# Long convolution and linear attention in one kernel: the second inverse step without its DRAM turn, x turned on TensorE, and a new order of all instructions

## The chip, the cores and the metric

The kernel runs on one core of one Trainium2 chip. The metric is device time in microseconds: 200.88 us, the median of three runs (199.52 to 201.84). The engines are PE (TensorE: matmul, with its weight loads as PEld), DVE (VectorE), ACT (ScalarE), POOL (GpSimd) and SP (SyncE, which here only issues transfers). They run side by side, each in the order of its own queue, and wait for each other through semaphores. SBUF is the on-chip memory, PSUM the eight banks of 512 fp32 columns that matmuls write.

## What is computed

Two independent parts, whose outputs lie side by side in the last dimension (S = 2048 rows, D = 576 channels each, bf16).

```python
# A: y = q * (causal_long_conv(kv, ssm_k) + kv * ssm_D)
k_shift = sum(k_pad[:, t:t + S] * shift_k[:, ks - 1 - t] for t in range(4))
kv = k_shift * v
y = irfft(rfft(pad(kv, 2*S)) * rfft(pad(ssm_k, 2*S)))[:S].astype(bf16)
a = q * (y + kv * ssm_D)
# B: linear attention, 32 heads of 18 channels
q, k, v = split(x @ wqkv)
pq, pk = phi(q), phi(k)          # phi(t) = (t + 1 if t > 0 else exp(t)) + 1e-6
kv, z = pk^T v, sum(pk)          # per head
b = (pq kv) / (pq z + 1e-6) @ wo
out = concatenate([a, b], axis=-1)
```

## The kernel before

**Part A** takes the channels in three groups of 192 (`cc`). `conv_piece` makes kv on DVE from shifted copies of k: two products with four taps (L383), sums (L388, L391), and the product with v (L394), for the two halves of the rows (`bh` 0 and 1). `h_piece` turns ssm_k on TensorE (L416). The Fourier transform of the filter ("h") and of kv ("u") goes in two steps. `s1` multiplies by the table `Gsb` (L445): each step fills three PSUM banks, 1,536 columns, which ACT or DVE copies to SBUF (`copy`, L246 to L250, so that all these copies stand under L248 for ACT and L250 for DVE). `s2` transposes 32x32 blocks on DVE (L463) and multiplies with the 16-point matrix W, as 32x32 matmuls on four row groups and four column groups of the array (L476), two PSUM banks a step; 64 channels at a time, so nine pieces `g`.

`inv` multiplies the two spectra on DVE (`p1` L503, `p2` L500, the second with the filter's real and imaginary rows exchanged by a transfer, `X`), and applies the first inverse step as 32x32 matmuls with W stationary (L513). Its result V has the frequency in the free dimension. `inv2` therefore writes V to DRAM (`v_scr`) and reads it back with the frequency on the partitions (`Vt`: four reads for every four row offsets, 32 in all), multiplies with the table `Esb` (L550), multiplies the PSUM result with q on DVE (L555), and stores. It does so in two halves, of 320 and 256 channels.

**Part B** loads x transposed with transposing transfers (L299, L302), projects k (`kproj`, L577; exp on ACT L582, phi on DVE L585) and q (`qproj`, L599, L603, L606: two PSUM banks, 1,024 rows a step, transposed as pqT). `b_G` forms x^T pk (L636), and from it come kv per head, z, the matrix M = kv wo (`b_M`) and the denominators for all heads and rows, one matmul group (L712). Their reciprocal is one DVE instruction (L723). It is spread over the 18 channels of each head by 20 small matmuls into PSUM (`b_bc`, L747) and multiplied into pqT on DVE (L753, ten times). `b_out` multiplies pqT with M for 16 tiles of 128 rows (L766), two PSUM banks each, copies (`oev`) and stores (`oo`).

**The order** is written out. Every call of `P.op` records one step, and `PLAN` lists the steps of all engines in one sequence, each with a letter for its engine (P, A, D, G = POOL, S = SP) and its number; `_issue` reads it. `PLACES` gives each buffer's address or PSUM bank. No engine looks ahead: a step that waits holds up all that stands behind it in its own queue. Every transfer of the kernel is issued by SP, and it also takes one of eight completion counters in turn, so that it is not issued before the eighth transfer ahead of it has landed.

The loads that the prediction speaks of: `kh0` holds rows of k in blocks of 16 per partition, with the three rows ahead of each block in the columns 0 to 2. These three rows are loaded apart (`khh`, L332 and L334), as 15 and as 112 partitions, and both for 192 and for 384 channels.

Of the kernel before, what the change touches and what calls it, by code (L numbers as in the profile page):

```python
# [14 lines left out]
D = 576  # L15
EPS = 1e-6
FT = [0, 128, 256, 384, 449]
HCH = [(0, 126), (126, 126), (252, 126), (378, 126), (504, 72)]
HEADS = [7, 7, 7, 7, 4]
CC = 192  # L20
NCC = 3
PCH = 64
VN = (320, 256)
VP = (0, 5)
HALF = 288

class Buf:

    def __init__(self, name, shape, dt=BF, space="sb", side=0, banks=0, pre=False):
        self.name, self.shape, self.dt, self.space = name, list(shape), dt, space
        self.side, self.banks, self.pre = side, banks, pre
        n = 1
        for d in shape[1:]:
            n *= d
        self.nbytes = -(-n * (4 if dt == FP32 else 2) // 32) * 32
        self.users = 0
        self.pos = None
        self.keys = {}  # L40
        self.t = None
# [6 lines left out]
class Prog:  # L48
# [11 lines left out]
    def op(self, engs, fn, rd=(), wr=(), name="", bias=0.0, tx=0.0, after=(), use=(), cnt=1):  # L60
        o = Op()
        o.id = len(self.ops)
        o.engs = engs if isinstance(engs, dict) else dict([engs])
        o.fn, o.name, o.bias, o.tx, o.cnt = fn, name, bias, tx, cnt
# [28 lines left out]
        for b in use:  # L93
            note(b)
# [3 lines left out]
        for b in bufs:  # L98
            b.users += 1
# [19 lines left out]
def _tables():  # L119
# [11 lines left out]
    pp = np.arange(128)  # L131
    k2p = 32 * (pp % 4) + pp // 4
    phe = ((4 * k2p[:, None, None] - 1) * n.T[None, :, :]) % 8192
    E = np.empty((128, 16, 2, 128), np.float32)
    E[:, :, 0, :] = np.cos(w0 * phe) / 2048.0
    E[:, :, 1, :] = -np.sin(w0 * phe) / 2048.0
# [17 lines left out]
    W[np.abs(W) < 1e-7] = 0.0  # L154

    C = np.zeros((128, 96 + 128 + 630 + 32 + 160 + 126 + 8), np.float32)
    o = 0
    C[:, 0:96] = np.tile(W.reshape(32, 96), (4, 1))
    o = 96
    C[:, o:o + 128] = np.eye(128)  # L160
    o += 128
    es = np.zeros((32, 5, 126), np.float32)
    hm = np.zeros((128, 5, 32), np.float32)
    for c, (h0, hn) in enumerate(HCH):
        for m in range(hn):
            es[7 * c + m // 18, c, m] = 1.0
            hm[m, c, 7 * c + m // 18] = 1.0
    C[:, o:o + 630] = np.tile(es.reshape(32, 630), (4, 1))
    o += 630
# [8 lines left out]
    return G.astype(bf), E.astype(bf), C.astype(bf)  # L178
# [10 lines left out]

def _pe(*ns):
    return sum(max(n / 2400.0, 0.026) + 0.0025 for n in ns)

def _act(n):
    return 0.17 + n * 0.000868

def _dve(n, rate=1):
    return 0.145 + n * 0.001045 / rate  # L200

def _dma(nb, row=4096):
    return nb / (16.0 * row / (8.0 + row * 0.0412) * 1000.0)
# [3 lines left out]
def kernel(  # L208
# [17 lines left out]
    Gt, Et, Ct = _tables()  # L226
    G_d = nc.inline_tensor(Gt.reshape(128, -1), name="tab_g").ap()
    E_d = nc.inline_tensor(Et.reshape(128, -1), name="tab_e").ap()
    C_d = nc.inline_tensor(Ct, name="tab_c").ap()

    V_d = [nc.dram_tensor("v_scr%d" % i, (128, 32 * VN[i]), BF, kind="Internal").ap() for i in range(2)]
# [7 lines left out]
    def dma(dst, src):  # L239
        nc.sync.dma_start(out=dst, in_=src)  # L240

    def load(name, b, fn, nb, wr=None, rd=(), bias=0.0, after=(), issue=0.45, row=4096):
        return P.op(("SP", issue), fn, rd=rd, wr=[b] if wr is None else wr, name=name, bias=bias,
                    tx=_dma(nb, row), after=after)

    def copy(e, o, i):  # L246
        if e == "ACT":
            nc.scalar.activation(out=o, in_=i, func=ACTF.Copy)  # L248
        else:
            nc.vector.tensor_copy(out=o, in_=i)  # L250

    def either(n, da=0.0, dd=0.0, rate=1):
        return {"ACT": _act(n) + da, "DVE": _dve(n, rate) + dd}
# [5 lines left out]
    cst = SB("cst", [128, Ct.shape[1]], side=1, pre=True)  # L259
    neg1 = SB("neg1", [128, 1], FP32, side=1, pre=True)  # L260
    Gsb = SB("Gsb", [128, 16, 2, 128], side=1, pre=True)
    Esb = SB("Esb", [128, 16, 2, 128], side=1)
# [3 lines left out]
    wk = SB("wk", [128, 5, D], side=1, pre=True)  # L266
    wq = SB("wq", [128, 5, D], side=1, pre=True)
    Drow = SB("Drow", [1, D], side=1)
    x_sb = SB("x_sb", [128, 16, D + 1], side=1)
    pk = SB("pk", [128, 16, D + 1], side=1, pre=True)  # L270
    pqT = SB("pqT", [128, 5, S], side=1, pre=True)
# [4 lines left out]
    W2 = lambda: cs(0, 32)  # L276
    W31 = lambda: cs(32, 32)
    W32 = lambda: cs(64, 32)
    ident = lambda: cs(96, 128)
    esel = lambda: cs(224, 630).rearrange("p (c m) -> p c m", c=5)  # L280
    sel127 = lambda: cs(854, 32)
    hmask = lambda: cs(886, 160).rearrange("p (c m) -> p c m", c=5)
    maskbd = lambda: cs(1046, 126)
    epsc = lambda: cs(1172, 1)

    P.op(("POOL", 0.1), lambda e: nc.gpsimd.memset(neg1.t[:], -1.0), wr=[neg1], name="neg1", bias=1000)
    for wx in (wk, wq):
        P.op(("POOL", 0.4), lambda e, wx=wx: nc.gpsimd.memset(wx.t[0:64, 4, :], 0.0), wr=[(wx, "z")], name="wz", bias=990)
        P.op(("POOL", 0.4), lambda e, wx=wx: nc.gpsimd.memset(wx.t[0:1, 4, :], 1.0), rd=[(wx, "z")], wr=[(wx, "z")],
             name="w1", bias=980)  # L290
# [3 lines left out]
    def xt_load(g):  # L294
        b = SB("xT%d" % g, [128, 5, 512])
# [5 lines left out]
        def f2(e):  # L301
# [580 lines left out]
```

## Time and profile before

The runs took 200.88, 201.84 and 199.52 us. The profiled execution has a span of 197.3 us from its first to its last instruction; its own time is not listed, so what lies around the span is taken as the 3.6 us to the median.

| what | value |
|---|---|
| median of three runs | 200.88 us |
| span of the profiled execution | 197.3 us |
| PE busy | 162.8 us, 83%, 1,664 matmuls |
| DVE busy | 153.4 us, 78%, 150 instructions |
| ACT busy | 120.0 us, 61%, 127 instructions |
| POOL busy | 6.9 us, memsets only |
| mean granted TensorE clock | 0.895 of full speed |
| transfers | 39.49 MB; SP alone issues |

A group of the profile has a source line, an engine, an operation, the tiles' names with their shapes, a count, and then the busy time and the mean duration of one; behind the second bar stands how long the engine was idle just before such instructions, and what ended that. In a row of stretches stand the stretch, its length, and per engine the busy time and number of instructions. The chain is followed back from the last instruction to what released each step.

### The profile page before, as it was taken

Reading aid. Unit: us, or ns where it says so; the run is one execution under the profiler, and the core shown is the slowest. Engines: PE = TensorE matmul, PEld = TensorE weight load, DVE = VectorE, ACT = ScalarE, POOL = GpSimd, SP = SyncE. Lnnn points to the kernel's source line nnn. Section 1 sums busy time; section 2 is a strip of 40 time slices with the busy share of each in tenths; the row PEclk is TensorE's granted clock in tenths of the full one; section 3 lists DMA queues with packets and bytes.
Section 4 is the critical chain, followed back from the end, with each engine's and each line's share of the span. In section 5 each row is a group of like instructions: output and inputs, shape, how many; then the busy total and the mean of one; then the engine's idle time right before and its main releaser. Section 6 shows DMA issues by size and latency. Waiting matters only on the chain.

```text
span 197.3 us, 3955 instructions
## 1 busy us (share of the span) xinstructions
PE 162.8 (83%) x1664; PEld 108.2 (55%) x1664; DVE 153.4 (78%) x150; ACT 120.0 (61%) x127; POOL 6.9 (3%) x18
## 2 busy tenths in 40 slices
PE   0985999938999999889998897798779999996820
PEld 0763576627666675668775564362233566774610
DVE  0477599999799999999954999979899548482650
ACT  2293566595767576997524699979998583201100
POOL 8010100020010000000000000000000000000000
PEclk9996699985999999999999999769555699999996
DMA  6999899996013680209950021930699789967696
GB/s 182 348 171 262 307 379 382 300 230 138 0 22 118 201 279 17 92 3 278 372 233 0 3 106 69 308 108 0 257 342 257 187 240 360 354 189 211 198 323 185
DMA packets 40536, 39.49 MB, mean 200 GB/s; under 512 B 13575, under 2 KB 37765, under 8 KB 39622
## 3 DMA queue, kind: packets, MB, share of 16 engines
q1 hardware_dynamic: 40518, 39.24, 64.7%
q8 instruction: 13, 0.21, 0.5%
q14 instruction: 5, 0.04, 0.1%
HBM read 22.46 MB, written 9.44 MB: 162 GB/s over the span
## 4 chain that ended last, share of the span: by engine, by line
PE 37%; DVE 24%; ACT 12%; SPq 11%; issue 7%; DMA 6%; DVEq 1%; ACTq 0%
PE ps_all L636 8%; SPq L240 7%; PE ps_all L599 6%; PE ps_all L577 6%; PE ps_all L766 6%; DVE m L383 5%; PE ps_all L445 5%; DMA Vt<-v_scr 3%; ACT Cu L248 3%; DVE X L500 3%; SPq L299 2%; DVE pk L585 2%; DVE ct L463 2%; DMA wk<-in_B_wqkv_dram 2%; PE ps_all L550 2%
## 5 line engine op out<-in xcount | busy, mean ns | idle before, releaser
L445 PEld LDWEIGHTS <-Gsb 128*128 128x128 bf16 x240 | 20.0, 113 | 11.2 <-issue 9.7
L577 PE MATMUL ps_all<-wk,xT 128*128 128x288 bf16 x160 | 23.4, 306 | 2.5 <-DMA wk<-in_B_wqkv_dram 2.5
L766 PE MATMUL ps_all<-M,pqT 126*128 126x288 bf16 (+1 forms) x160 | 23.5, 305 | 0.2 <-ACT V L248 0.2
L599 PE MATMUL ps_all<-xT,wq 128*126 128x512 bf16 (+1 forms) x100 | 23.5, 386 | 0.1
L383 DVE TENSOR_TENSOR m<-kh,Wj 128x3072 bf16<-128x3072 bf16 x12 | 20.7, 1750 | 1.9 <-DMA kh<-in_A_k_dram 1.9
L577 PEld LDWEIGHTS <-xT 128*128 128x128 bf16 x160 | 16.4, 104 | 9.3 <-issue 3.6
L766 PEld LDWEIGHTS <-pqT 126*128 126x128 bf16 (+1 forms) x160 | 16.4, 103 | 7.5 <-issue 2.2
L636 PE MATMUL ps_all<-pk,x_sb 128*128 128x288 bf16 (+1 forms) x160 | 20.4, 286 | 0.1
L248 ACT ACTIVATE sph<-ps_all 128x1024 bf16<-128x1024 f32 x16 | 16.2, 1028 | 4.4 <-PE ps_all L476 4.4
L248 ACT ACTIVATE spu<-ps_all 128x1024 bf16<-128x1024 f32 x16 | 15.9, 1028 | 4.7 <-PE ps_all L476 4.7
L248 ACT ACTIVATE Cu<-ps_all 128x1536 bf16<-128x1536 f32 x12 | 17.5, 1502 | 1.1 <-PE ps_all L445 1.0
L582 ACT ACTIVATE ek<-ps_all,neg 128x576 bf16<-128x576 f32 x16 | 11.8, 741 | 10.5 <-PE ps_all L577 6.9
L636 PEld LDWEIGHTS <-x_sb 128*128 128x128 bf16 x160 | 15.5, 98 | 4.8 <-issue 0.9
L599 PEld LDWEIGHTS <-wq 128*126 128x126 bf16 (+1 forms) x100 | 13.1, 135 | 8.3 <-issue 1.3
L248 ACT ACTIVATE Ch<-ps_all 128x1536 bf16<-128x1536 f32 x11 | 16.1, 1523 | 2.5 <-PE ps_all L445 2.3
L248 ACT ACTIVATE ob<-ps_all 128x576 bf16<-128x576 f32 x10 | 6.5, 652 | 17.7 <-PE ps_all L766 17.3
L445 PE MATMUL ps_all<-hT,Gsb 128*128 128x192 bf16 (+2 forms) x120 | 12.8, 272 | 5.3 <-DVE hT L425 3.4
L476 PE MATMUL ps_all<-ct,cst 32*32 32x512 bf16 x288 | 13.2, 438 | 4.0 <-ACT Cu L248 0.9
L603 ACT ACTIVATE eq<-ps_all,neg 126x1024 bf16<-126x1024 f32 (+1 forms) x10 | 11.1, 1114 | 7.8 <-PE ps_all L599 7.8
L248 ACT ACTIVATE V<-ps_all 128x1024 bf16<-128x1024 f32 x14 | 13.7, 1035 | 2.7 <-PE ps_all L513 2.7
L555 DVE TENSOR_TENSOR q<-ps_all,q 128x640 bf16<-128x640 f32 (+1 forms) x12 | 11.0, 953 | 5.5 <-PE ps_all L550 4.6
L585 DVE SCALAR_TENSOR_TENSOR pk<-ek,ps_all 128x576 bf16<-128x576 bf16 x16 | 11.6, 746 | 3.7 <-ACT ek L582 2.0
(69 smaller groups left out, 224.1 us busy)
## 6 DMA issues: line engine op xcount, KB each, us to landing
X<-sph SPq DMA_DIRECT2D x18, 256.0 KB, 2.8
v_scr<-V SPq DMA_DIRECT2D x1, 2560.0 KB, 10.0
Vt<-v_scr SPq DMA_DIRECT2D x16, 160.0 KB, 3.5
hs<-in_A_ssm_k_dram SPq DMA_DIRECT2D x6, 384.0 KB, 5.6
v<-in_A_v_dram SPq DMA_DIRECT2D x2, 1152.0 KB, 11.1
x_sb<-in_B_x_dram SPq DMA_DIRECT2D x1, 2304.0 KB, 9.5
out_dram<-ob SPq DMA_DIRECT2D x16, 144.0 KB, 3.3
v_scr<-V SPq DMA_DIRECT2D x1, 2048.0 KB
```

What stands on the lines that cost most here:

```text
L240: nc.sync.dma_start(out=dst, in_=src)
L248: nc.scalar.activation(out=o, in_=i, func=ACTF.Copy)
L383: nc.vector.tensor_tensor(out=m.t[:, i:i + 2], in0=i0, in1=i1, op=ALU.mult)
L445: nc.tensor.matmul(ps.t[:, bank, lo - 512 * bank:hi - 512 * bank], lhsT=Gsb.t[:, b, ri, :], rhs=src[:, lo - CC * j:hi - CC * j], start=Tru ...
L476: nc.tensor.matmul(ps.t[32 * j:32 * j + 32, kk, :].rearrange("p (k w t) -> p w k t", w=8, t=2), lhsT=W2()[32 * kh:32 * kh + 32, :], rhs=ct ...
L577: nc.tensor.matmul(ps.t[:, hh, 0:HALF], lhsT=xT.t[:, t, 128 * (r % 4):128 * (r % 4) + 128], rhs=wk.t[:, t, HALF * hh:HALF * hh + HALF], st ...
L582: P.op(("ACT", _act(576) + 0.085), lambda e: nc.scalar.activation(out=eb.t[:], in_=ps.t[:, :, 0:HALF], func=ACTF.Exp, bias=neg1.t[:]), rd= ...
L585: P.op(("DVE", _dve(576)), lambda e: nc.vector.scalar_tensor_tensor(out=pk.t[:, r, 0:D].rearrange("p (h c) -> p h c", h=2), in0=eb.t[:], s ...
L599: nc.tensor.matmul(ps.t[0:hn, j, :], lhsT=wq.t[:, t, h0:h0 + hn], rhs=xT.t[:, t, :], start=(t == 0), stop=(t == 4))
L603: P.op(("ACT", _act(1024) + 0.09), lambda e: nc.scalar.activation(out=eb.t[0:hn], in_=ps.t[0:hn], func=ACTF.Exp, bias=neg1.t[0:hn, :]), rd ...
L636: nc.tensor.matmul(ps.t[:, hh, 0:n], lhsT=x_sb.t[:, r, FT[t]:FT[t] + 128], rhs=pk.t[:, r, HALF * hh:HALF * hh + n], start=(r == 0), stop=( ...
L766: nc.tensor.matmul(ps.t[:, hh, 0:HALF], lhsT=pqT.t[0:hn, c, 128 * r:128 * r + 128], rhs=M.t[0:hn, c, HALF * hh:HALF * hh + HALF], start=(c ...
```

## The change

`PLAN` and `PLACES` are new, and the steps between them are cut otherwise:

- `s1`, `s2`, `qproj`, `b_G` and `b_out` work in smaller PSUM steps: two banks of 384 columns in `s1`, one bank elsewhere. There are twice as many copies, each of half the size.
- `inv` makes the spectral products the stationary operand, 128 frequencies by 128 columns at a stride of 16, and multiplies with W repeated four times on the diagonal (two more blocks at the end of `Esb`). The result comes out with the frequency on the partitions. The DRAM tensor, its writes and its read-backs are gone. `inv2` takes three groups of 192 channels; for the first two a copy goes ahead of the product with q.
- x is loaded untransposed in four parts, turned by 80 TensorE transposes, and copied to `xT`. The row order inside a tile becomes 16 p + r, for x and for the output.
- The reciprocal is written to DRAM as (head, two copies, row) and read back five times, each row nine times over, into one tile per head group; pqT is multiplied by it in five DVE instructions. The small constant of phi is no longer added to each element there: the plain reciprocals are read into rows 96 to 127 of the last pqT tile, and M gets 32 more rows, the sums of its heads' rows times 1e-6 (`smm`, 10 matmuls).
- Some conv sums and products (`tap+`, `tapv`), four `p1` and three products with q run on POOL. Three early loads are issued by ACT.
- k's three rows ahead are one transfer of 127 partitions.

```diff
-            for ci, (c0, cn) in enumerate(((0, CC), (CC, D - CC))):
-                load("khh", kh, lambda e, c0=c0, cn=cn: dma(kh.t[1:16, 0:3, c0:c0 + cn], ap(
-                    k, 13 * D + c0, [[16 * D, 15], [D, 3], [1, cn]])), 90 * cn, wr=[(kh, (ci, "h1"))], row=2 * cn)
-                load("khh", kh, lambda e, c0=c0, cn=cn: dma(kh.t[16:128, 0:3, c0:c0 + cn], ap(
-                    k, 253 * D + c0, [[16 * D, 112], [D, 3], [1, cn]])), 672 * cn, wr=[(kh, (ci, "h2"))],
...
+            load("khh", kh, lambda e: dma(e, kh.t[1:128, 0:3, :].rearrange("p a d -> p (a d)"), ap(k, 13 * D, [[16 * D, 127], [1, 3 * D]])),
+                 438912, 3456, wr=[(kh, "h")])
+            load("kh0", kh, lambda e: dma(e, kh.t[:, 3:11, :].rearrange("p a d -> p (a d)"), ap(k, 0, [[16 * D, 128], [1, 8 * D]])),
+                 1179648, 9216, wr=[(kh, "m")])
...
-        def f1(e):
-            nc.sync.dma_start_transpose(out=b.t[:, 0:4, :], in_=x[512 * g:512 * g + 512, 0:512])
...
+        for t0, tn in ((0, 2), (2, 2), (4, 1)):
+            ps = psb(1, "xps")
+            def tr(e, t0=t0, tn=tn, ps=ps):
+                o = ps.t.rearrange("p b c -> p (b c)").bitcast(BF)
+                for j in range(tn):
+                    for i in range(4):
+                        nc.tensor.transpose(out=o[:, 512 * j + 128 * i:512 * j + 128 * i + 128],
+                                            in_=x_sb.t[:, 4 * g + i, FT[t0 + j]:FT[t0 + j] + 128], identity=ident())
...
-            for bg in range(2):
-                ps = psb(3, "s1ps")
+            for bg in range(4):
+                ps = psb(2, "s1ps")
...
-        for kp in range(2):
-            ps = psb(2, "s2ps")
+        for kh in range(4):
+            ps = psb(1, "s2ps")
...
-                for wi, (w, src) in enumerate(((W31, tx), (W32, xb))):
-                    for kh in range(4):
-                        for jj in range(2):
-                            j = 2 * jp + jj
-                            nc.tensor.matmul(ps.t[32 * kh:32 * kh + 32, jj, :],
-                                             lhsT=w()[32 * j:32 * j + 32, :],
-                                             rhs=src.t[32 * j:32 * j + 32, kh, :],
-                                             start=(wi == 0), stop=(wi == 1))
+                for c8 in range(4):
+                    for wi, src in ((0, tx), (1, xb)):
+                        nc.tensor.matmul(o[:, 128 * c8:128 * c8 + 128],
+                                         lhsT=view(src.t[:], 4 * hh + c8, [[16, 128]]),
+                                         rhs=Esb.t[:, 32 + wi, :], start=(wi == 0), stop=(wi == 1))
...
-        load("Vw", None, lambda e: dma(vd, V[hf].t[:].rearrange("p k c -> p (k c)")), 8192 * n, rd=[V[hf]], wr=[dtok],
...
-                    load("Vr", vt, lambda e, b4=bg * nb, vt=vt, kh=kh: dma(
-                        vt.t[kh:128:4], ap(vd, (32 * kh + 2 * b4) * 32 * n, [[n, 32], [32 * n, 8], [1, n]])),
...
+                        nc.tensor.matmul(ps.t[:, 0, n * j:n * j + n], lhsT=Esb.t[:, 2 * b + ri, :], rhs=V[gi].t[:, 2 * b + ri, :],
+                                         start=(ri == 0), stop=(ri == 1))
...
+                P.op("AD", lambda e, yv=yv, yb=yb, bg=bg: copy(e, yb.t[:, nb * (bg % 2):nb * (bg % 2) + nb], yv()),
...
+                    P.op("DG", mul2, rd=[yb, (qb, "q")], wr=[(qb, (gi, bg - 1)), (qb, (gi, bg))], name="yq", n=2 * nb * n, x2=1, two=1, st=st)
...
-                nc.tensor.matmul(ps.t[0:hn, j, :], lhsT=esel()[32 * g:32 * g + 32, c, 0:hn],
-                                 rhs=rden.t[32 * g:32 * g + 32, :], start=True, stop=True)
...
+    for i in range(2):
+        load("rw", None, lambda e, i=i: dma(e, ap(r_d, i * S, [[512, 4], [2 * S, 32], [1, 512]]), rden.t[:]), 131072, 1024,
+             rd=[rden], wr=[(rtok, i)])
+    for c, (h0, hn) in enumerate(HCH):
+        rb = SB("rb", [128, S])
+        load("rr", rb, lambda e, c=c, hn=hn, rb=rb: dma(e, rb.t[0:hn, :], ap(r_d, 14 * c * S, [[S, hn // 9], [0, 9], [1, S]])),
+             4096 * hn, 4096, rd=[rtok])
+        P.op("D", lambda e, c=c, hn=hn, rb=rb: tt(e, pqT.t[0:hn, c, :], pqT.t[0:hn, c, :], rb.t[0:hn, :], ALU.mult),
+             rd=[rb], wr=[(pqT, (c, g)) for g in range(4)], name="pqn", n=2048, x2=1, two=1)
+    load("rh", None, lambda e: dma(e, pqT.t[96:128, 4, :], ap(r_d, 0, [[2 * S, 32], [1, S]])), 131072, 4096, rd=[(rtok, 0)], wr=[(pqT, "r")])
...
-        ps = psb(2, "ops")
+        for hh in range(2):
+            ps = psb(1, "ops")
```

In the new list SP issues, after the tables and the first loads: `khh`, `kh0`, the body of `wq`, `v0`, `wv`, `cst`, and then the first exchange `X`. DVE's first conv product stands behind 21 shorter DVE steps, and the first q tile on PE behind eleven steps of `htr`, ten of `xtr`, eight of `s1`, six of `kproj` and eight of `s2`. The first output tile comes after all nine inverse pieces.

More of the change, by code (lines that the diff above doesn't have):

```diff
@@ L273, in cs @@
+    ident = lambda: idw.t[:, 0:128]
+    W2 = lambda: idw.t[:, 128:160]
     def cs(o, n):
         return cst.t[:, o:o + n]
[L276 to L286, printed above, removed]
@@ L623 @@
-    P.op(("POOL", 0.3), lambda e: nc.gpsimd.memset(x_sb.t[:, :, D:D + 1], 1.0), wr=[(x_sb, "o")], name="x1",
-         bias=400, after=[k_ids[AFTER["x"]]])
+    for g in range(4):
+        for c in range(5):
+            qproj(c, g)
     GT = SB("GT", [128, 5, D])
```

681 lines of the change are left out of this document (326 added, 355 removed), and 27 rows, old and new, of the table PLACES.

## The prediction

> **What bounds the kernel now.** First the page's busy times, then the stretches, cut where the chain changes its engine.
>
> ```profile
> PE 162.8 (83%) x1664; PEld 108.2 (55%) x1664; DVE 153.4 (78%) x150; ACT 120.0 (61%) x127; POOL 6.9 (3%) x18
> ```
>
> ```profile
> 28.00:150.00 122.00, 108.48 (x1201) 70.50 (x1209) 112.27 (x107) 93.17 (x97) 1.79 (x4) 0.90 0.53 166
> 150.00:188.40 38.40, 35.02 (x342) 23.84 (x333) 23.87 (x26) 13.01 (x17) 0.00 (x0) 0.92 0.80 247
> 0.00:28.00 28.00, 19.34 (x140) 13.88 (x141) 15.43 (x18) 13.77 (x13) 5.07 (x14) 0.88 0.93 271
> 188.40:197.30 8.90, 0.00 (x0) 0.00 (x0) 1.77 (x2) 0.00 (x0) 0.00 (x0) 0.79 0.83 247
> ```
>
> Columns: stretch, length, busy us (and instructions) of PE, PEld, DVE, ACT, POOL, clock, DMA share, GB/s. No engine's average says it, but the stages do. From 28 to 150 us DVE is busy 112 of 122 us: that stage is DVE's, with PE at 89% and ACT at 76%. From 150 to 188 PE is the busy one (output tiles and the second inverse step). The last 8.9 us are stores alone. In the chain of work that ended last, in order of time, that third stage waits twice for the DRAM turn, behind some eight issues of the SP queue each time:
>
> ```profile
> 162.16 3.77 DMA Vt<-v_scr
> ...
> 178.53 2.58 DMA Vt<-v_scr
> ```
>
> The prices below come from these groups (line, engine, shapes, count | busy, mean ns | idle before):
>
> ```profile
> L383 DVE TENSOR_TENSOR m<-kh,Wj 128x3072 bf16<-128x3072 bf16 x12 | 20.7, 1750 | 1.9 <-DMA kh<-in_A_k_dram 1.9
> L248 ACT ACTIVATE Cu<-ps_all 128x1536 bf16<-128x1536 f32 x12 | 17.5, 1502 | 1.1 <-PE ps_all L445 1.0
> L248 ACT ACTIVATE sph<-ps_all 128x1024 bf16<-128x1024 f32 x16 | 16.2, 1028 | 4.4 <-PE ps_all L476 4.4
> L513 PE MATMUL ps_all<-sph,cst 32*32 32x512 bf16 x144 | 7.9, 431 | 1.7 <-ACT V L248 0.8 <-ACT Cu L248 0.4 <-DVE sph L503 0.3
> L248 ACT ACTIVATE ob<-ps_all 128x576 bf16<-128x576 f32 x10 | 6.5, 652 | 17.7 <-PE ps_all L766 17.3 <-ACT ob L248 0.4
> L503 DVE TENSOR_TENSOR sph<-spu,sph 128x2048 bf16<-128x2048 bf16 x9 | 10.8, 1215 | 0.4 <-ACT spu L248 0.4
> L394 DVE TENSOR_TENSOR v<-m,v 128x1536 bf16<-128x1536 bf16 x6 | 5.6, 939 | 0.0
> L655 POOL MEMSET wv<- 128x576 bf16 x1 | 0.6, 582 | 15.2 <-PE ps_all L599 15.2
> ```
>
> ACT's rows lie on a line: 652 ns for 576 columns, 1,028 for 1,024, 1,502 for 1,536, so 0.82 us for 768, 0.60 for 512, 0.50 for 384 and 0.42 for 288. On DVE likewise 0.94, 0.68, 0.55 and 0.45.
>
> **The edits, priced.**
> - *One-bank steps.* First transform: 48 evictions of 768 columns for 24 of 1,536 (ACT 39 x 0.82 = 32, DVE 9 x 0.94 = 8.5; before 33.6 + 1.8): +5 us. Second transform: 72 of 512 for 36 of 1,024 (64 x 0.60 + 8 x 0.68 = 43.8; before 36.9): +7. The q exponentials: 20 x 0.69 (1,114 less 427) = 13.8, before 11.1. Nearly all of it is ACT's.
> - *Inverse.* 288 matmuls of 32x32, in groups of 16 at some 0.6 us (11 us), become 288 of 128x128. The trace has no such one; a 128-column one with its own weights starts 56 ns after the last (in L445's group), and transposes whose weights are read at the same stride of 16 elements 62 ns (L416). Between 56 and the 80 ns of the slower transposes I take 62: 17.9 us, +7. 36 evictions of 512 (22.0 us) for 18 of 1,024 (18.5): +3.5. The second step keeps its columns (96 x 192); 16 of its 24 results now go through an eviction (14 on ACT, 7.0 us) before the product with q, so that POOL can do 3 of 8 products. The DRAM write, its 32 read-backs and the 6.4 us of the chain above go.
> - *x on TensorE.* 8 transposing DMAs and their queue time (up to 5.4 us each) go; 80 transposes at about 60 ns (5 us PE) and 12 evictions (ACT 5.9, DVE 3.2) come.
> - *Reciprocals.* 20 broadcast matmuls (5.1 us busy) go, and 10 products of 1.21 us become 5. A chain comes: 3.35 us of reciprocal, two writes, five reads, five products. By 3.3 us for a write (the issues' row of out<-ob) and 3.5 for a read (Vt<-v_scr), five issues of 0.6 and the q load ahead of it in the SP queue, it takes some 20 us from the denominators to the first output tile. Each engine has about 20 us of listed work in between: it costs nothing, but it is late next.
> - *To POOL* go 4 + 4 conv steps, 4 products and 3 q products: DVE loses 14 us. POOL's price is unknown: 0.94 us for 1,536 columns (DVE's row) at the least, 4.6 at the most (1.0 ns per column of its memset, for each of three streams). I take 3.5; the consumers come 7 us or more behind in the list.
> - *Stores.* 384-byte rows (22 ns a packet in the trace): 8.4 us over 16 engines, beside 6.5 us for the 1,152-byte ones, under 26 us of output stage: hidden.
>
> **A wait nobody named.** Before loads the three rows of k ahead of each block as 15 + 112 partitions; now it is one transfer of 127 partitions of 3,456 bytes. The landings in the trace show on how many DMA engines a transfer runs: 16 counts for 128 rows, 14 for the 126 rows of wo, 12 for its 72, 15 for the 15 rows of k, 1 for the single row of srow. All divide the row count; 127 is prime, so one engine. The Trainium skill says this in "DMA: Bandwidth & Descriptors", section "Why a DMA increments its semaphore by 16 and not by 1": the largest number up to 16 that divides both row counts, its example 127 giving 1. By it, as by the landings, the sum stands as below; without it, it is 14 us less.
>
> A packet takes 51 ns at 1,152 bytes and 164 at 4,096, so 139 at 3,456: 127 x 139 = 17.7 us on that one engine, against 8 x 139 = 1.1. Ahead of it the engine has its share of six hs (5.9), four x parts (6.5), Gsb (2.5), wk (1.6) and small ones (0.6): 17 us from about 2.2, so 19.3 to 37.0. Behind it on the same engine wait kh0 (8 x 352 ns: 39.8) and wq (41.4). DVE's first conv product needs kh0, and DVE has only 16 us of work listed ahead of it; PE's first q tile needs wq, with some 21 us of PE work ahead from 5 us on. Both queues are in order: DVE stands from about 24 to 41 us, PE from about 28 to 42, ACT behind them. Were the load spread, this would be at 25 to 28.
>
> **The sum**, for the profiled execution (span 197.3; median of three runs 200.88, so 3.6 us around it):
> 1. To the first conv product: 41.
> 2. From there to the first output tile: DVE has 122.8 us of rows (taps 21.0, their sums 12.4, q and k 22.6, transposes 18.3, spectral products 16.9, evictions 16, normalising 6.0, reciprocal 3.4, rest 6), ACT 126.2, PE about 109 at full clock. In 28 to 150 before, DVE's durations add up to 119.2 in 122 us (neighbours overlap a little), with PE and ACT (99.2) in reserve. At that rate ACT's 126.2 would take 126 to 129. Now three queues are full at once, and each waits for the others: 138, if the fullest reaches only 92%. I take 132.
> 3. Output tiles: 160 x 123 ns plus four last i2 groups 1.3 = 21, at 95%: 22 (before 38.4).
> 4. Last eviction, issue and landing (3.3): 4.4 (before 8.9).
>
> 41 + 132 + 22 + 4.4 = 199.4; with the 3.6: **203 us**, 1% slower. The change gains 16 in the third stage, 4.5 in the last, and gives back 13 at the head and 10 in the middle.
>
> **Rivals.**
> - *The middle keeps before's pace* (126): 193.4 + 3.6 = 197, faster. One mechanism: ACT's short evictions overlap their neighbours (6.1 us over 97 instructions there before), so twice as many lose nothing to their fixed part. It decides once ACT's 126 us shrink under DVE's 123. For it: PE waited for ACT only some 7 us in all before. Against: three equal queues.
> - *The 127-row load is spread or covered*: 14 us less, 189. Against it is every landing count in the trace.
> - *DVE and POOL stand in each other's way*, and the list's order breaks: 12 POOL steps, some 46 us, beside DVE's two-input products (61 of 123 us). If DVE has such a product next half of the time and then waits for half a POOL step, 12 x 0.5 x 1.9 = 11 us: 203 + 11 = 214, and 207 at a third of that. The trace has no POOL step but memsets. The Trainium skill, "SBUF — State Buffer", section "Who interferes with whom", says that a VectorE instruction with two SBUF inputs and a reading GpSimd one block each other, the second one wholly; no run here shows it yet, and by it this rival's time holds.
>
> **Numbers.** Measured differences under about 1% say nothing here. Forecast 0.36 (199 to 208); before's pace 0.24 (193 to 199); spread or covered 0.13 (185 to 192); POOL and broken order 0.27 (207 to 216). Faster by over 1% (under 198.9) 0.35, within 0.15, slower 0.50. The range that leaves out 2 in 10: 188 to 214; the forecast's own is 199 to 208.
>
> **What would show it.** A stall of PE and DVE ending near 41 us, released by the kh0 and wq loads, with one landing of the 127-row load; ACT over 140 us busy; no wait for v_scr; the gap from the last matmul to the end under 6 us; POOL steps of 2 to 5 us. I am wrong if both engines run through 25 to 42 us, or if the middle takes under 125 or over 140 us.

## The result and the profile after

The changed kernel takes 211.68 us (median of four runs, 210.50 to 212.07) beside 201.16 us for the kernel before in the same session: a ratio of 1.058, interval 1.051 to 1.065. It is slower by 5.8%. The forecast was 203.0 with a range of 188 to 214. The direction is right and the range holds the time; the forecast itself is 8.7 us too low. The profiled execution took 210.5 us, 208.5 of them in its span.

A cut at three events of the work shows where the time went. They are the first and the last of the twelve conv products of kh and Wj on DVE (L360 after, L383 before), and the first matmul of an output tile (L724 after, L766 before). All values are us of one profiled execution; the middle two columns are what the prediction called the middle.

| kernel | to first conv product | first to last conv product | to first output tile | to the end of the span | span |
|---|---|---|---|---|---|
| before | 11.0 | 75.5 | 64.6 | 46.2 | 197.3 |
| after | 47.5 | 67.9 | 66.0 | 27.1 | 208.5 |
| predicted | 41 | 132 together | | 26.4 | 199.4 |

The output stage gave 19 us, of 20.5 expected for it and the end, the conv stretch gave 7.6, and the head took 36.5: the kernel before has its first conv product at 11.0 us, the changed one at 47.5. (The prediction cut the kernel before at 28 us, which is none of these events. By the same events its 41 and 132 us mean a head 30 us longer than before and the next two stretches 8 us shorter; they came out 36.5 longer and 6.2 shorter.) Here and below a ratio goes against the kernel before, run beside each kernel; a median takes in every run, while the ratio leaves disturbed ones out and decides.

The page of the changed kernel, its busy times:

```profile
PE 165.7 (79%) x1718; PEld 126.0 (60%) x1718; DVE 149.8 (72%) x167; ACT 133.0 (64%) x237; POOL 57.7 (28%) x36
```

Then its stretches, cut at those events, and six pieces of the first half (columns as in the prediction's second fence: busy us of PE, PEld, DVE, ACT, POOL, granted clock, DMA share, GB/s):

```profile
0.00:47.50 47.50, 25.55 (x280) 21.18 (x280) 14.92 (x21) 20.47 (x30) 8.13 (x19) 0.95 0.76 230
47.50:115.40 67.90, 63.60 (x545) 41.83 (x546) 64.25 (x67) 55.65 (x91) 25.75 (x10) 0.91 0.19 70
115.40:181.40 66.00, 53.25 (x719) 45.41 (x717) 58.25 (x55) 49.62 (x98) 23.82 (x7) 0.93 0.46 146
181.40:208.50 27.10, 23.35 (x178) 17.55 (x176) 12.36 (x27) 7.27 (x19) 0.00 (x0) 0.92 0.58 175
15.00:20.00 5.00, 2.45 (x28) 2.46 (x29) 0.00 (x0) 0.74 (x2) 0.00 (x0) 1.00 1.10 352
20.00:25.00 5.00, 4.96 (x53) 4.57 (x52) 4.12 (x6) 4.46 (x7) 1.47 (x5) 1.00 0.71 168
25.00:30.00 5.00, 4.79 (x60) 3.71 (x58) 4.80 (x7) 3.77 (x8) 0.00 (x0) 1.00 0.21 48
40.00:45.00 5.00, 0.00 (x0) 0.00 (x0) 0.00 (x0) 0.00 (x0) 0.00 (x0) 0.73 0.47 151
45.00:50.00 5.00, 0.00 (x0) 0.18 (x1) 2.49 (x2) 0.00 (x0) 0.00 (x0) 0.50 0.43 154
50.00:55.00 5.00, 3.54 (x10) 1.43 (x10) 4.89 (x6) 1.53 (x3) 1.12 (x1) 0.50 0.06 21
```

From 40 to 45 us no engine computes at all. The trace has the granted clock at 0.50 from 42.3 to 59.4 us. In the conv stretch DVE is busy 64.3 of 67.9 us, and before 69.5 of 75.5:

```profile
11.00:86.50 75.50, 66.16 (x543) 45.93 (x542) 69.49 (x67) 53.22 (x54) 2.81 (x6) 0.91 0.65 185
```

The chain of waits that ended last, in order of time (start, length, what):

```profile
19.09 28.30 DMA kh<-in_A_k_dram
...
51.46 2.29 PE ps_all L566 x5
...
158.73 4.22 DMA r_scr<-rden
...
165.61 8.99 DMA rb<-r_scr
...
181.99 3.54 PE ps_all L724 x14
```

The load of kh is the longest piece of the whole chain. The 127 packets of 3,456 bytes stand in the trace one behind the other, with a median of 135 ns, from 24.0 to 44.1 us, and that load landed at 44.6. Eight packets of kh0 (9,216 bytes) follow in the same way to 46.9. Of the 16 completions of kh0, 15 had come by 34.8 and the last came at 47.4: this one released DVE. The load held more than its own DMA engine. SP's two issues of kh, the 127 rows and then kh0, are

```profile
18.77 10.23 SPq L214 DMA_DIRECT2D kh<-in_A_k_dram  x2
```

9.9 us of this are the issue of kh0 (0.4 with the load spread, below), and the body of wq is issued only behind it, at 29.0. So from 24.5 to 28.5 us, and again from 43 to 45, the mean busy share of the 16 DMA engines is 0.06 to 0.07, which is one engine's worth. No wait for v_scr is left; in its place stands the new chain of the reciprocals, a write of 4.2 us and reads of 9.0.

The groups of the changed kernel that answer to those in the prediction (busy us, mean ns of one, idle us before):

```profile
L360 DVE TENSOR_TENSOR m<-kh,Wj 128x3072 bf16<-128x3072 bf16 x12 | 20.6, 1752 | 13.0 <-DMA kh<-in_A_k_dram 12.9
...
L221 ACT ACTIVATE sph<-ps_all 128x512 bf16<-128x512 f32 x35 | 19.2, 611 | 0.1
...
L221 ACT ACTIVATE V<-ps_all 128x512 bf16<-128x512 f32 x31 | 18.6, 705 | 1.6 <-PE ps_all L479 1.6
...
L221 ACT ACTIVATE Cu<-ps_all 128x768 bf16<-128x768 f32 x21 | 17.5, 871 | 3.2 <-PE ps_all L413 2.6 <-DVE ct L433 0.7
...
L228 DVE TENSOR_TENSOR sph<-spu,sph 128x2048 bf16<-128x2048 bf16 x5 | 9.9, 2003 | 0.0
...
L221 ACT ACTIVATE ob<-ps_all 128x288 bf16<-128x288 f32 x19 | 7.3, 410 | 24.0 <-PE ps_all L724 24.0
```

The conv products cost what they did, but DVE stood 12.9 us for kh. The copies came out near their estimates (0.61, 0.87 and 0.41 us for 0.60, 0.82 and 0.42), apart from V, which is read in one order and written in another: 0.705. A spectral product on DVE now takes 2.0 us in the mean where it took 1.2.

### The profile page after: what moved, and what is told of

It reads as the page before. It is cut to its first block, busy times and chain, and to the rows that moved or that the text cites. A ratio compares the mean times of both kernels' runs of the same rounds, so it can differ in the third digit from the quotient of the medians.

```text
span 208.5 us, 4202 instructions
## 1 busy us (share of the span) xinstructions
PE 165.7 (79%) x1718; PEld 126.0 (60%) x1718; DVE 149.8 (72%) x167; ACT 133.0 (64%) x237; POOL 57.7 (28%) x36
## 4 chain that ended last, share of the span: by engine, by line
PE 34%; DMA 27%; DVE 20%; issue 8%; ACT 6%; SPq 2%; DVEq 0%; POOL 0%; ACTq 0%
DMA kh<-in_A_k_dram 14%; PE ps_all L724 10%; DMA x_sb<-in_B_x_dram 7%; DVE m L360 5%; DMA rb<-r_scr 4%; PE ps_all L594 4%; PE ps_all L479 4%; PE ps_all L566 4%; PE ps_all L413 4%; DVE ct L433 3%; DVE pqT L572 3%; DVE m L228 3%; PE ps_all L443 2%; SPq L214 2%; DMA r_scr<-rden 2%
## 5 line engine op out<-in xcount | busy, mean ns | idle before, releaser
L566 PE MATMUL ps_all<-xT,wq 128*126 128x512 bf16 (+1 forms) x100 | 26.8, 407 | 12.6 <-DVE hT L223 12.6
L360 DVE TENSOR_TENSOR m<-kh,Wj 128x3072 bf16<-128x3072 bf16 x12 | 20.6, 1752 | 13.0 <-DMA kh<-in_A_k_dram 12.9
L228 POOL TENSOR_TENSOR m<-m 128x1536 bf16<-128x1536 bf16 x4 | 12.4, 3098 | 53.0 <-DVE m L228 53.0
L566 PEld LDWEIGHTS <-wq 128*126 128x126 bf16 (+1 forms) x100 | 12.9, 139 | 21.3 <-DMA wq<-in_B_wqkv_dram 10.4
L228 POOL TENSOR_TENSOR sph<-spu,sph 128x2048 bf16<-128x2048 bf16 x4 | 17.0, 4261 | 27.1 <-ACT spu L221 15.8
L724 PE MATMUL ps_all<-M,pqT 126*128 126x288 bf16 (+1 forms) x160 | 22.5, 300 | 0.1
L594 PE MATMUL ps_all<-pk,x_sb 128*128 128x289 bf16 (+1 forms) x160 | 22.3, 294 | 0.1
L550 ACT ACTIVATE ek<-ps_all,neg 128x576 bf16<-128x576 f32 x16 | 11.9, 747 | 16.2 <-DVE pk L553 12.6
L479 PE MATMUL ps_all<-Esb,sph 128*128 128x128 bf16 x144 | 20.1, 227 | 0.0
L479 PE MATMUL ps_all<-Esb,X 128*128 128x128 bf16 x144 | 20.0, 226 | 0.0
L221 ACT ACTIVATE V<-ps_all 128x512 bf16<-128x512 f32 x31 | 18.6, 705 | 1.6 <-PE ps_all L479 1.6
L221 ACT ACTIVATE Cu<-ps_all 128x768 bf16<-128x768 f32 x21 | 17.5, 871 | 3.2 <-PE ps_all L413 2.6
L221 ACT ACTIVATE sph<-ps_all 128x512 bf16<-128x512 f32 x35 | 19.2, 611 | 0.1
L479 PEld LDWEIGHTS <-sph 128*128 128x128 bf16 x144 | 18.8, 149 | 0.8 <-issue 0.8
L724 PEld LDWEIGHTS <-pqT 126*128 126x128 bf16 (+1 forms) x160 | 16.1, 102 | 5.2 <-DVE pqT L228 0.6
L479 PEld LDWEIGHTS <-X 128*128 128x128 bf16 x144 | 18.5, 149 | 0.2 <-issue 0.2
```

The costliest lines, as they stand in the source:

```text
L228: (nc.vector if e == "DVE" else nc.gpsimd).tensor_tensor(out=o, in0=a, in1=b, op=op)
L360: nc.vector.tensor_tensor(out=m.t[:, i:i + 2], in0=i0, in1=i1, op=ALU.mult)
L479: nc.tensor.matmul(o[:, 128 * c8:128 * c8 + 128], lhsT=view(src.t[:], 4 * hh + c8, [[16, 128]]), rhs=Esb.t[:, 32 + wi, :], start=(wi == 0) ...
L550: P.op("A", lambda e: nc.scalar.activation(out=eb.t[:], in_=ps.t[:, :, 0:HALF], func=ACTF.Exp, bias=neg1.t[:]), rd=[ps, neg1], wr=[eb], na ...
L566: nc.tensor.matmul(ps.t[0:hn, 0, :], lhsT=wq.t[:, t, h0:h0 + hn], rhs=xT.t[:, t, :], start=(t == 0), stop=(t == 4))
L594: nc.tensor.matmul(ps.t[:, 0, 0:n], lhsT=x_sb.t[:, r, FT[t]:FT[t] + 128], rhs=pk.t[:, r, HALF * hh:HALF * hh + n], start=(r == 0), stop=(r ...
```

## The experiments

A row of four or five numbers has the columns of the first table.

### One part of the change alone, in the kernel before

```diff
-load("khh", kh, lambda e, c0=c0, cn=cn: dma(kh.t[1:16, 0:3, c0:c0 + cn], ap(
-    k, 13 * D + c0, [[16 * D, 15], [D, 3], [1, cn]])), ...
-load("khh", kh, lambda e, c0=c0, cn=cn: dma(kh.t[16:128, 0:3, c0:c0 + cn], ap(
-    k, 253 * D + c0, [[16 * D, 112], [D, 3], [1, cn]])), ...
+load("khh", kh, lambda e, c0=c0, cn=cn: dma(kh.t[1:128, 0:3, c0:c0 + cn], ap(
+    k, 13 * D + c0, [[16 * D, 127], [D, 3], [1, cn]])), ...
```

> The kernel before, and of it only the loads of k's three rows ahead as 127 partitions instead of 15 and 112, once for 192 channels (381 packets of 384 bytes) and once for 384 (381 of 768). At 22 ns for a packet of 384 bytes and some 35 for 768, one engine has 8.4 and 13 us for them. Theory 1, the row count decides: the first conv product moves from 11.0 us to 16 to 20, the loads behind are late by up to 20 us on that engine, and the time rises by 6 to 20 us, to 206 to 220. Theory 2, the loads spread over more engines whatever the row count: within 1% of before.

Measured: 217.47 us, ratio 1.091 (1.079 to 1.104). Row: 17.7, 89.2, 64.6, 45.1, span 216.6. Theory 1 holds: the first conv product moved from 11.0 to 17.7, as expected, and the rest of the loss lies in the conv stretch, in loads that queue up after the second slow one. From its waits (who waited for what: us in all, times, longest):

```profile
PE ps_all L598 <- DMA wq<-in_B_wqkv_dram: 13.5, 1, 13.5
...
PE ps_all L415 <- DMA hs<-in_A_ssm_k_dram: 12.3, 2, 7.0
```

Here too SP stands right behind each of the two slow loads, in its issue of Drow and of the tail of wq (from the chain; 0.2 and 1.2 us in the kernel before):

```profile
2.01 7.56 SPq L240
...
27.50 16.15 SPq L240
```

The two stages behind the last conv product are what they were. This one edit costs the kernel before 18 us, more than the whole change costs.

### The same part undone, in the changed kernel

```diff
-  dma(e, kh.t[1:128, 0:3, :], ap(k, 13 * D, [[16 * D, 127], [1, 3 * D]]))
+  for p0, pn in ((1, 15), (16, 112)):
+      dma(e, kh.t[p0:p0 + pn, 0:3, :], ap(k, (16 * p0 - 3) * D, [[16 * D, pn], [1, 3 * D]]))
```

> The changed kernel with k's three rows ahead loaded as 15 and as 112 partitions again; nothing else differs. In the changed kernel's profile the 127-row load lands at 47.4 us; DVE stands from 34.5 to 47.5 (12.9 us) and PE from 38.9 to 51.5 for it. Theory 1, the one-engine load holds both queues and what it costs is kept to the end: 211.7 less 11 to 13, so 199 to 201, and the first conv product at 34 to 37 us. Theory 2, other queues take the time back (POOL beside DVE, the reciprocals, the loads behind): the first conv product comes early, but the end only by 3 to 8, so 204 to 209. Theory 3, the block of loads as a whole is late and the row count decides nothing: within 1% of 211.7.

Measured: 194.93 us, ratio 0.985 (0.976 to 0.993): far below the changed kernel, and some 1.5% below the kernel before. Row: 35.7, 65.5, 64.4, 27.4, span 193.0. Theory 1, with more than it asked: 15.5 us of span. Of these, 11.8 are at the first conv product. SP's issues of kh, now three, take 1.3 us in all:

```profile
19.45 1.32 SPq L214 DMA_DIRECT2D kh<-in_A_k_dram  x3
```

Another 2.4 are in the conv stretch, and the chain of waits of this kernel shows why. Its first q tile and its first output tiles are

```profile
40.09 1.08 PE ps_all L569 x5
...
166.16 3.54 PE ps_all L727 x14
```

Five q matmuls take 1.08 us here and 2.29 in the changed kernel, where PE had stood for 12.6 us and the clock was granted at 0.50. In the changed kernel DVE then idles 2.75 us for the exponentials of the second q tile, beside 1.09 with the spread load. This stall of PE is paid twice: while it lasts, and at half clock behind it, here 2.3 us over the first two q tiles. (The Trainium skill, "TensorE: Matmul & The Clock Gate", section "Part 1: The HAM clock gate", says that the array falls to half its clock after an idle window of about 3.4 us and needs about as long a busy one to come back; the trace agrees on the half and on the fall, at 42.3 us, 3.4 after PE's last matmul ended, while the full clock came back only 7.9 us after PE had started again.)

### All POOL steps on DVE, without and with the spread load

```diff
-... G577 ... G656 ... G635 ... G693 ... G772 ... G790 ... G748 (and eight conv steps)
+... D577 ... D656 ... D635 ... D693 ... D772 ... D790 ... D748 (and eight conv steps)
```

> The changed kernel with all 15 two-input POOL steps (4 + 4 conv sums and products, 4 spectral products, 3 products with q) on DVE, at the same places of the list. By the rows these are 8 x 0.94 + 4 x 1.21 + 3 x 0.55 = 14.0 us more listed work for DVE. Theory 1, DVE and POOL block each other: the products of 2,048 columns that ran beside POOL took 1.95 to 2.0 us in place of 1.21 (nine of them), nine others 1.45, and DVE stood for 4.7, 2.5, 2.1, 1.5 and 1.0 us right before two-input products for nothing that the profile shows: about 20 us lost, more than the 14 that POOL takes over, so 203 to 209 us, and all two-input rows of DVE back at 1.21. Theory 2, POOL relieves DVE and the losses lie beside other waits: 217 to 226 us. Theory 3, DVE sets neither: within 1% of 211.7.

> Both edits: k's three rows as 15 and 112 partitions, and the 15 POOL steps on DVE. If the two losses are apart, the time is the changed kernel's less the two single gains. If DVE is the bound of the middle once the stall is gone, the POOL steps are worth their 14 us: 8 to 14 us slower than the spread load alone. If the blocking is worth more than the relief: 2 to 6 us faster than the spread load alone, so 193 to 197 us.

Measured: 210.50 us, ratio 1.064 (1.054 to 1.074), row 47.9, 75.2, 59.3, 25.5; and with the spread load 196.04 us, ratio 0.992 (0.986 to 0.997), row 34.6, 73.0, 58.3, 25.9. Theory 3 of the first run by the totals: within 1% of the kernel with POOL, in both cases. Not for the reason it gave. Of the second run's three cases none holds: it is 1.1 us slower than the spread load alone, where 8 to 14 slower and 2 to 6 faster were the numbers, and the two single gains added would have given 193.7. With the spread load the conv stretch grows by 7.5 us, just the eight steps of 0.94 us that POOL had taken from DVE; the next stretch shrinks by 6.1, though DVE has 6.5 us more listed work in it. There the blocking is seen directly. The timeline of the kernel with the spread load has, on DVE and on POOL:

```profile
104.00 2.75 DVE L228 TENSOR_TENSOR m<-m 128x3072 bf16<-128x3072 bf16 x2
106.67 5.10 DVE L228 TENSOR_TENSOR sph<-spu,sph 128x2048 bf16<-128x2048 bf16 x1
111.69 1.21 DVE L228 TENSOR_TENSOR X<-spu,X 128x2048 bf16<-128x2048 bf16 x1
...
105.93 4.76 POOL L228 TENSOR_TENSOR sph<-spu,sph 128x2048 bf16<-128x2048 bf16 x1 [5.27 <-ACT spu L221]
```

POOL's product starts at 105.93 and ends at 110.69. The product that DVE starts at 106.67 ends 1.1 us after that, about its own length: it waited for the whole of POOL's. With the steps on DVE, all nine such products take 1.21 us. This is the rule of the Trainium skill that the prediction cited ("SBUF — State Buffer", "Who interferes with whom"), and the rows agree with "wholly". The conv steps of POOL ran beside copies and other instructions with one SBUF input, and there nothing on DVE was longer than elsewhere (q's 512 columns 0.64 to 0.69 us beside them, 0.67 in the mean of the group).

### Short memsets ahead

```diff
-G221 S7 G1 G6 ... S18 ... G5 ... G13 ... G2 ... G3 ... G4
+G5 G1 G2 G3 G4 G0 G13 G221 G6 G50 S7 ... S18 ...
```

> The spread load, and POOL's short memsets ahead of the first transfers: the ones column of x, the ends of wk and wq. In the changed kernel the memset of x's ones column stands behind the first part of x (POOL idle 3.7 us, to 9.0), the tail of wk behind that (issued at 9.9 instead of 6), and with it the other three parts of x (10.6 to 11.7), which land at 17.5; PE is busy 7.1 of the first 20 us. Theory 1, this order of memsets delays the head: x is there 3 to 4 us sooner and the whole is 2 to 4 us faster than the spread load alone. Theory 2, the loads are bound by their bytes (the DMA engines are over 90% busy from 2 to 27 us): within 1 us of the spread load alone.

Measured: 194.88 us, ratio 0.984 (0.974 to 0.993); row 32.2, 67.0, 67.3, 26.3, span 192.8. The mechanism of theory 1 is there (the first conv product is 3.5 us earlier), the total is that of theory 2. The 3.5 us are given back behind it, 1.5 in the conv stretch and 2.9 in the next one. So what the late start of x costs at the head isn't, as the list stands, a cost of the kernel.

### Ten to twelve microseconds more for one engine

Each of three kernels adds work to one engine of the kernel with the spread load and leaves the results as they are. The work isn't added in one place: DVE's lies in the conv stretch, PE's in the inverse step behind it, and ACT's in both.

```diff
-copy(e, sp.t[:, kh, :], ps.t[:, 0, :])                                   # ACT: e5_halves
+[copy(e, sp.t[:, kh, 256 * i:256 * i + 256], ps.t[:, 0, 256 * i:256 * i + 256]) for i in range(2)]
-for wi, src in ((0, tx), (1, xb)):                                       # PE: e11_pe
+for wi, end, src in ((0, True, tx), (0, False, tx), (1, True, xb)):
-nc.vector.tensor_tensor(out=m.t[:, i:i + 2], in0=i0, in1=i1, op=ALU.mult)  # DVE: e12_dve
+for _ in range(2 if i == 0 else 1):
+    nc.vector.tensor_tensor(out=m.t[:, i:i + 2], in0=i0, in1=i1, op=ALU.mult)
```

> The kernel with the spread load (194.9 us), and each of the 72 copies of 512 columns after the second transform step cut into two of 256. By ACT's line (0.40 us for 256 columns, 0.61 for 512) 64 of them on ACT cost 0.19 more each, 12 us more ACT work, and 8 on DVE 1.5 us. Theory 1, the queues of the middle are all full and ACT's short copies are on the path, as the 132 us of the middle assumed: 6 to 12 us slower, 201 to 207. Theory 2, ACT has slack there (it is busy 133 of 193 us) and PE and DVE set the pace: under 3 us slower, 195 to 198.

> The kernel with the spread load and 144 matmuls of 128x128 too many in the first inverse step (each first one of a pair is done twice, with the same result), at 70 ns some 10 us of TensorE between 118 and 160 us. Theory 1, PE sets the pace there (busy 9.5 to 10 of every 10 us): 8 to 11 us slower, 203 to 206. Theory 2, PE's busy time there is waiting for the copies' banks: under 4 us slower.

> The kernel with the spread load and six DVE products of 3,072 columns too many (the first of the two tap products of each piece done twice, with the same result): 6 x 1.75 = 10.5 us of DVE between 36 and 101 us. Theory 1, DVE sets the pace there (busy 9.6 to 10 of every 10 us), as in the kernel before: 8 to 11 us slower, 203 to 206. Theory 2, its queue has slack against PE's: under 4 us slower. With 12 us more of ACT the time rose by 2.4 us.

| added | median us | ratio | row |
|---|---|---|---|
| nothing | 194.93 | 0.985 (0.976 to 0.993) | 35.7, 65.5, 64.4, 27.4 |
| ACT, 64 copies, some 12 us expected | 197.29 | 0.996 (0.991 to 1.002) | 34.0, 67.5, 67.0, 26.2 |
| PE, 144 matmuls, some 10 us expected | 197.57 | 0.978 (0.968 to 0.988) | 34.0, 67.0, 65.7, 26.6 |
| DVE, 6 products, 10.5 us | 207.05 | 1.042 (1.032 to 1.051) | 36.6, 76.0, 65.9, 26.6 |

DVE passes its 10.5 us on whole: its conv stretch is 10.5 longer, the total 12 (theory 1). DVE sets the pace there; that it did so in the kernel before rests on its busy share alone. PE, the busiest engine of the page, passes on little or nothing (theory 2): by the median of all ten runs 2.6 us, by the ratio nothing. Its busy time rose by 5.3 us only, so it too was asked less than meant, and the conv stretch, where PE is busy 65.1 of 65.5 us, wasn't asked. The run on ACT came out at 2.3 us, theory 2 by its number, but it put a smaller question than it meant to: ACT's busy time rose from 132.5 to 136.2 us, 3.7 instead of 12. A copy of half the size costs far less extra than the line through single copies says when the next follows at once. What ACT's real time is worth is thus not settled by it; that short copies in a row are cheap is.

### The reciprocals sooner: two trials

The first forms the group of x^T pk that z needs before the others, puts the denominators some 130 steps sooner, and the five reads ahead of the load of q.

```diff
-    for t in range(5):
+    for t in (4, 1, 2, 3, 0):
         b_G(t)
...
 PLAN: z, denominators, reciprocal, writes ~130 steps sooner; five reads ahead of qld
```

> The kernel with the spread load, and the reciprocals earlier: the group of x^T pk that holds z is formed first of the five instead of last, the denominators follow some 130 steps sooner in the list (their matmuls, the sum, the reciprocal, the two writes), and the five reads go ahead of the load of q. With the spread load alone PE stands between 157 and 166 us and the first output tile starts at 166.2, released by the last product with the reciprocals. Theory 1, the chain of reciprocal, write, five reads and products sets the first output tile: 5 to 8 us faster than 194.9, so 187 to 190, with no wait of DVE for the reads. Theory 2, the inverse pieces and M are hardly earlier: 0 to 3 us faster, 192 to 195.

Measured: 198.57 us, ratio 0.996 (0.991 to 1.002); row 35.2, 65.5, 66.2, 29.8. It is slower than the spread load alone by 1 to 2%, which neither theory held. DVE now stood at the new place of the denominators (busy 5.4 of 10 us from 110 to 120), and q, behind the reads in SP's queue, landed at 168.7 us, after the first output tile at 166.9; the products with q then held the output stage. The trial moved the wait instead of taking it away.

The second leaves the groups in order and q ahead of the reads.

```diff
 PLAN: z, denominators, reciprocal ~65 steps sooner, behind the last group's copy
-... S86 ... S236 ... S237 ... S246 ... S242 S244 ... S238 ... S240 ... S248
+... S236 S237 ... S86 S246 S242 S244 S238 S240 S248   # the reads right behind the load of q (S86)
```

> The kernel with the spread load, and the reciprocals earlier in a milder way: the five groups of x^T pk stay in their order; z, the denominators and the reciprocal follow as soon as the last of them is copied (some 65 steps sooner, 8 to 10 us), and the five reads stand right behind the load of q instead of ahead of it. The first trial of this kind held DVE for 5.4 us at the denominators' step (DVE busy 5.4 of 10 us between 110 and 120) and let q land at 168.7 us. Theory 1, the chain of reciprocal, write, reads and products sets the first output tile: 4 to 7 us faster than 194.9, so 188 to 191, the first output tile at 159 to 162. Theory 2, it hides another wait (the last inverse pieces, M): 0 to 2 us.

Measured: 189.51 us, ratio 0.956 (0.946 to 0.964). Row: 35.1, 65.5, 62.5, 24.8, span 187.9. Theory 1 in size: 5.4 us faster than the spread load alone. Of the span's 5.1 us, 2.5 are won by the first output tile, which starts at 163.1 in place of 165.6 (the theory had 159 to 162), and 2.6 behind it, where PE no longer starts at half clock, which the theory didn't have:

```profile
163.25 1.85 PE ps_all L727 x15
```

Fifteen matmuls in 1.85 us, beside fourteen in 3.54 in the two kernels where PE had stood.

### Only the short steps on POOL

In the kernel of the second trial, the four spectral products and three products with q go to DVE and the eight conv steps stay on POOL (the seven letters G of the diff above).

> The kernel of the second trial with the reciprocals (189.5 us), with the four spectral products of 2,048 columns and the three products with q moved from POOL to DVE; the eight conv steps of 1,536 columns stay on POOL. With all 15 steps on DVE the stretch from the first to the last conv product grew from 65.5 to 73.0 us, but the one from there to the first output tile shrank from 64.4 to 58.3, though DVE had 6.5 us more listed work in it. Theory 1, the long POOL steps block DVE's own spectral products and cost more than they take over, the conv steps do not: the conv stretch stays at 65.5, the next one shrinks by 3 to 6, 183.5 to 186.5 us. Theory 2, the earlier reciprocals have already filled that loss: within 2 us of 189.5.

Measured: 189.26 us, ratio 0.950 (0.938 to 0.962); row 37.5, 65.5, 61.1, 24.4 for an execution of 190.6 us, whose head is 2.4 longer though nothing there was changed. Theory 2: no difference that can be measured; the stretch behind the conv products shrinks by 1.4, not by 3 to 6. The blocking is gone (groups of this kernel: busy us, mean ns),

```profile
L228 DVE TENSOR_TENSOR sph<-spu,sph 128x2048 bf16<-128x2048 bf16 x9 | 10.8, 1209 | 0.0
L228 DVE TENSOR_TENSOR X<-spu,X 128x2048 bf16<-128x2048 bf16 x9 | 10.8, 1215 | 0.0
```

and little is won by it: what blocking took and what POOL relieved nearly cancel each other, here as in the pair above.

### A miss

> The changed kernel with the 127-row load as it is, but issued first of all transfers. Theory 1, one DMA engine works its queue in order: 127 x 0.135 = 17 us on it come before its share of every other load, so no transpose of the filter or of x starts before 18 to 20 us instead of 5, but DVE and PE do not stand later; 205 to 215 us. Theory 2, the engine takes turns between transfers and the load hides under the others: as the spread load, 195 to 198.

This kernel didn't put the question: the step that its list moved to the front was the load of wk's body, not the 127-row load.

```diff
-G221 S7 G1 G6 ... S10 G3 S46
+S46 G221 S7 G1 G6 ... S10 G3
```

The 127-row load was issued at 20.0 us, the first conv product started at 47.3, and the time was 209.96 us, ratio 1.043 (1.025 to 1.061), about that of the changed kernel. Whether the load could be hidden by issuing it first wasn't tried.

## Why the prediction came out as it did

**The 127-row load: right in kind, 6.5 us short in its place.** One engine, 127 packets of 135 ns (139 predicted), kh0 behind them on it, both queues standing for it, DVE's wait ended by kh: all as said. (PE's wait was ended by a copy of hT that stood behind the conv products on DVE, at 51.5; wq was there at 49.0.) The first conv product came at 47.5 instead of 41. The step that failed is "17 us from about 2.2, so 19.3 to 37.0". The first packet started at 24.0, the last ended at 44.1. SP issued the load only at 18.8 us, but that isn't the reason: the DMA engines were busy without a break from 2 to 23 us (mean share 1.0 to 1.1 in the rows from 5 to 20 us; packets overlap), so there was no room for it earlier. What was ahead of it took longer, 22.5 us on each engine instead of 17: the packets of hs 249 ns in the mean (164 were taken), those of x and the weights 60 (51), those of Gsb 396 (314). And the 127 packets took 20.1 us, not 17.7, since those that ran beside other loads took up to 308 ns. The sum went by the medians of the kernel before. The packets beside busy engines are longer, and the trace of before had this too: 207 ns in the median for 4,096 bytes in its first 30 us.

The engines came later to the wait as well (DVE at 34.5 instead of 24, PE at 38.9 instead of 28), so each stood 13 us, not 14 to 17. Three of the four parts of x had waited until 9 to 11 us: a memset of one column of x stood behind the first part, and the tail of wk in SP's queue behind POOL's memsets. The first of them was there at 17.5, and DVE's work ahead of the first conv product began in earnest at 20.4. The undoing gave 15.5 us of span where 14 were predicted: 11.8 at the head, and the rest behind it, 2.4 of it in the conv stretch with the half clock, which the prediction left out.

**The middle: 133.9 for 132, by other causes.** The closeness is luck. The reason given for 132 over the 126 of before's pace was ACT's 126.2 us, with three queues full at once, and that step failed. The price of a copy was right (0.61, 0.87 and 0.41 us), but ACT was busy 105.3 us in the middle, not 126.2: 20.5 us of its work lay ahead of the first conv product, under the stall. "ACT over 140 us busy" came out as 133.0. The engine nearest its limit is DVE, with 122.5 us busy in the middle. That 122.8 were predicted is luck too: the 122.5 hold 9 us of blocking by POOL's steps (2.2 on X, 4.0 on sph, 2.9 on pqT, over 1.21 us each), which the sum had at nothing. Without the stall the two stretches take 129.9; the half clock behind it goes with 2.4 more, and the reciprocals take about 2 of what is left.

**The reciprocals: "it costs nothing, but it is late next" failed.** The sum gave 20 us from the denominators to the first output tile. It took 28 (153.2 to 181.4): 3.3 for the reciprocal, then 4.2 for the write, 9.0 for the last reads where 3.5 was taken from reads of another size, five products at 1.80 us in place of 1.21. The cover of "about 20 us of listed work" had run out: between 170 and 180 us PE was busy 3.0. With the spread load, having them sooner was worth 5.4 us.

**Output stage and end: right.** 23.5 and 3.6 us for 22 and 4.4; the first of it at half clock (3.54 us for 14 matmuls).

**The rivals.** The case that the load is spread would have given 189; measured with the spread load, 194.9. The gap is the head, 35.7 where 27 was implied, and 1 in the output stage, less 2 in the middle and 1.7 around the span. POOL and DVE do block each other, and the time of that rival, 207 to 214, holds 211.7. But it is not its cause: taking the 15 steps off POOL (the rival counted 12) leaves the time within 1%. What the prediction priced as 1% slower is 5.8% slower mainly because of the head: 6.5 of the 8.7 us that the forecast lacked lie there, 1.9 in the middle.

**What stays open.** Why the 3.5 us of an earlier head are given back isn't shown. One thing stands in that trace: the granted clock was 0.50 from 32.7 to 36.1 us, where ten matmuls of k's projection took 2.60 us instead of 1.39, though PE had not stood before; whether that is part of it wasn't tried. It isn't shown either why SP stands in an issue behind a 127-row load, nor what holds PE between 110 and 120 us with the spread load (busy 6.3 of 10 us). How much of the 126 us of before's pace the changed middle could reach wasn't tried.

## What to carry to other kernels

Before a load is merged, look at its number of rows: two loads of 127 rows, each on one engine, cost a kernel 18 us that the same bytes as 15 and 112 rows didn't, two thirds of them in the loads that stood behind them. Price the packets ahead of a load by what they take when all engines are busy. Price a stall of TensorE with the half clock that follows it, and a chain of small transfers by its own sizes rather than by reads of another shape. And ask, stage by stage, which engine passes on its time by giving it more work: the second busiest engine of the page passed on its ten microseconds in full in the conv stretch, while the busiest passed on little or nothing of its five behind it.

## What the runs showed of the hardware that was not expected

- Behind a stall of 12.6 us TensorE ran at a granted clock of 0.50 for 7.9 us (2.29 us for five matmuls that take 1.08), and again behind the wait before the output tiles (3.54 us for 14 matmuls, beside 1.85 for 15).
- A product on DVE with both inputs in SBUF, started during such a step on POOL, ended only 1.1 us after POOL's: 5.10 us for 1.21. POOL itself took 3.10 us for 1,536 bf16 columns and 4.1 to 4.8 for 2,048.
- While one DMA engine worked through a 127-row load, SP stood in its next issues: 9.9 us for that of kh0, 0.4 with the load spread, and 7.6 and 16.2 us in the kernel before with two such loads. The other 15 DMA engines ran dry meanwhile (mean share of the 16: 0.06 to 0.07).
- While all DMA engines were busy, packets of 4,096 bytes took 249 ns in the mean, beside a median of 164 over the whole of the kernel before.
- A copy by ACT from PSUM that writes 512 columns in another order than it reads them took 0.705 us, where the plain one took 0.611.
